# An attention, expert and ELU feed-forward chain: score tiles on both partition halves, paired transposes, smaller softmax joins, values in three parts

## The chip, the core and the metric

The kernel runs on one core of a Trainium2 chip. The metric is the device time of one execution in microseconds. The engines named below are PE (matrix products; PEld is its loading of weights), DVE (VectorE), ACT (ScalarE), POOL (GpSimd) and SP, whose queue issues most of the transfers.

## What is computed

```python
# attention: q, k, v are (2, 8, 1152, 64)
q_pool = q.reshape(B, H, S // 2, 2, D).mean(axis=3)
scores = scale * np.matmul(q_pool, k.transpose(0, 1, 3, 2))
attn = np.exp(scores - np.max(scores, axis=-1, keepdims=True))
attn = attn / (np.sum(attn, axis=-1, keepdims=True) + 1e-09)
x = np.matmul(attn, v)                      # becomes (1152, 512)
# four experts, weighted
for e in range(4):
    out += p[:, e:e + 1] * (np.maximum(x @ w1[e], 0.0) @ w2[e])
# feed-forward with ELU
h = out @ w_in
g = np.where(h > 0.0, h, np.exp(np.minimum(h, 0.0)) - 1.0)
return g @ w_out
```

There are 16 heads; each has 576 pooled queries and 1152 keys. The two dense stages work on 1152 tokens of 512 features.

## The kernel before

**Two stages.** The attention stage comes first; the dense stage (experts, then ELU layer) follows and uses the attention's result as split pairs `XH` and `XL` (a high part and the remainder). This change touches the attention stage alone.

**Pairs and units.** Heads are taken in 8 pairs `p`; `y` (0 or 1) is the head within the pair. The 576 queries of a head are cut so that a unit `(p, u, y)` with `u` from 0 to 8 holds 64 queries: 32 of the lower and 32 of the upper half (`z`). So a pair has 18 units. A unit's scores lie on all 128 partitions as (z, a, 32 queries), where `a` picks one of two halves of the keys, and on 2 x 288 columns (`n`), in two banks' worth of one score buffer `s`. There are three such buffers.

**The steps.** The planner names each step with a letter:

- `k`, `q`, `v`: loads, issued by SP (the first q by ACT); `a` adds the two queries that are pooled, `b` scales them.
- `S` scores (PE, 8 products of 64 rows by 32 columns, 288 keys each); `R` maximum of a unit (DVE); `E` exponential with its row sum (ACT), which reads the score buffer, writes an `e` buffer and frees the score buffer.
- The join. Each query has its keys on two partitions (`a`), so maximum and sum must be joined: `x` copies the partner's numbers across, `y` takes the smaller negated maximum, `Y` the differences, `e` their exponentials, `z` the whole sum, `r` its reciprocal, `g` the factor. A join is made for a group of units at a time.
- `G` multiplies a unit's 576 columns of `e` by its factor (POOL or ACT), `T` transposes it in blocks of 32 into `pt` (DVE), `V` multiplies by the values (PE, 72 products for a group), `O` and `L` write `XH` and `XL` (ACT, DVE).

In the kernel before, the groups are `GROUPS = ((0, 5), (5, 9))`: units 0 to 4 and 5 to 8 of a pair, 10 and 8 units with both heads. Join and values use the same groups. A head `y` sits on partitions 64y to 64y+63 of the k and q tiles, so all 8 products of one unit use one half of PE's rows, and the two column halves `n` of a unit follow one another on the same four tiles of the array. There are 14 `e` buffers, each for one unit.

**What sets the order.** `order_of` simulates the engines with the costs in `STAGES` and the latencies in `LAG`, and writes every step to its engine in the order of the start that it finds. The engines then run their lists strictly in order. What a step waits for is in `attention_ops`: `S` needs a score buffer freed by an `E`; `E` needs an `e` buffer freed by the `T` of 14 units earlier; `V` needs all `T` of its group; the `T` of a group needs the `V` of the same group one pair earlier. At the end of the stage four blocks of the first dense product (`1`, with `2` and `3` behind it) are mixed in; the planner's tail and `h`, `f` (conversion of the first weights) belong to the same list.

Of the kernel before, what the change touches and what calls it, by code (L numbers as in the profile page):

```python
# [18 lines left out]
P = 128  # L19
# [8 lines left out]
    "q": (dict(SP=500), 0),  # L28
    "k": (dict(SP=500), 0),
    "v": (dict(SP=1000), 2),  # L30
    "a": (dict(POOL=830, DVE=470), 0),
    "b": (dict(ACT=440, POOL=500), 0),
    "S": (dict(PE=560), 0),
    "R": (dict(DVE=750), 0),
    "E": (dict(ACT=960), 0),
    "x": (dict(ACT=860), 0),
    "y": (dict(DVE=175), 0),
    "Y": (dict(POOL=450), 0),
    "e": (dict(ACT=220), 0),
    "z": (dict(POOL=680), 0),  # L40
    "r": (dict(DVE=180), 0),
    "g": (dict(POOL=220), 0),
    "G": (dict(POOL=760, ACT=700), 0),
    "T": (dict(DVE=670), 1),
    "V": (dict(PE=5200), 0),
    "O": (dict(ACT=420), 0),
    "L": (dict(DVE=340), 0),
# [11 lines left out]
NU = 9  # L59
NE = 14  # L60
NG_ST = 4
GROUPS = ((0, 5), (5, 9))

# [4 lines left out]
def attention_ops(NP):  # L68
# [15 lines left out]
    for p in range(NP):  # L84
        b = 2 * NU * p
        old = [("S", *u) for u in units(p - 2)] if p > 1 else []
        for z in (0, 1):
            op(b - 20, old, "k", p, z, after=1000 * z)
            op(b - 20, old, "q", p, z, after=1000 * z)
            op(b - 14, [("q", p, z)], "a", p, z)  # L90
            op(b - 14, [("a", p, z)], "b", p, z)
        for y in (0, 1):
            op(b - 10, [("V", *g) for g in groups(p - 2)] if p > 1 else [], "v", p, y, after=4000)
        for gi, (lo, hi) in enumerate(GROUPS):
            g = (p, gi)
            r = 2 * NU * p + 2 * hi
            old = groups(p - 1)[gi] if p else None
            us = units(p, gi)
            for u in us:
                r0 = b + 2 * u[1] + u[2]  # L100
                op(r0, [(x, p, z) for x in "kb" for z in (0, 1)], "S", *u)
                op(r0, [("S", *u)] + ([("g", *old)] if old else []), "R", *u)
                before_e.append(u)
                op(r0, [("R", *u)] + ([("T", *before_e[-1 - NE])] if len(before_e) > NE else []), "E", *u)
            op(r, [("E", *u) for u in us], "x", *g)
            op(r, [("x", *g)], "y", *g)
            op(r, [("y", *g)], "Y", *g)
            op(r, [("Y", *g)], "e", *g)
            op(r, [("e", *g)], "z", *g)
            op(r, [("z", *g)], "r", *g)  # L110
            op(r, [("r", *g)], "g", *g)
            for j, u in enumerate(us):
                op(r + 0.9 * j, [("g", *g)], "G", *u)
                op(r + 0.9 * j, [("G", *u)] + ([("V", *old)] if old else []), "T", *u)
            op(r + 8, [("T", *u) for u in us] + [("v", p, y) for y in (0, 1)], "V", *g)
            for z in (0, 1):
                op(r + 8, [("V", *g)], "O", *g, z)
                op(r + 8, [("O", *g, z)], "L", *g, z)
# [18 lines left out]
def order_of(ops):  # L137
# [12 lines left out]

    while ready:
        best = []
        for o, t in ready.items():
            x = takes.get(o[0])
            if x:
# [3 lines left out]
            _, e = min((max(t, free[e]) + n, e) for e, n in STAGES[o[0]][0].items())  # L159
# [3 lines left out]
        free[e] = start + STAGES[o[0]][0][e]  # L163
        end[o] = free[e] + LAG[e]
        x, bank = takes.get(o[0]), None
        if x:
# [8 lines left out]
        elif o[0] == "L" and ("L", *o[1:3], 1 - o[3]) in end:  # L175
            back = ("V", *o[1:3])
# [13 lines left out]
def attention_then_moe_then_elu_ffn(  # L190
# [124 lines left out]
    with ExitStack() as actx:  # L315
# [13 lines left out]
        et = [e_p.tile([P, CB * 32], F32, name="e%d" % j) for j in range(NE)]  # L329
# [7 lines left out]
        def load_k(e, p, z):  # L337
            if p not in kt:
                kt[p] = kq_p.tile([P, KC * P], F32, tag="k", name="k")
            t = kt[p][:, z * KQ : z * KQ + KQ]  # L340
            for y in (0, 1):
                r = slice(64 * y, 64 * y + 64)
                if p == 0:
                    nc.sync.dma_start(out=t[r], in_=qk0[4 * y + 2 * z + 1, r])
                else:
                    src = kT[p // HP, p % HP].rearrange("(z d) y s -> z y d s", z=2)
                    nc.sync.dma_start(out=t[r], in_=src[z, y])  # L347

        def load_q(e, p, z):
            if p not in qs:  # L350
                qs[p] = kq_p.tile([P, 2, 2, HQ], F32, tag="q", name="q")
            t = qs[p][:, z].rearrange("p m s -> p (m s)")
            for y in (0, 1):
                r = slice(64 * y, 64 * y + 64)
                if p == 0:
                    nc.scalar.dma_start(out=t[r], in_=qk0[4 * y + 2 * z, r])
                else:
                    src = qT[p // HP, p % HP].rearrange("(z d) y m s -> z y d (m s)", z=2)
                    nc.sync.dma_start(out=t[r], in_=src[z, y])

        def load_v(e, p, y):
            vt[p, y] = t = v_p.tile([P, CB, D], F32, tag="v%d" % y, name="v")
            src = v[p // HP, 2 * (p % HP) + y].rearrange("(r t) c d -> r (t c d)", t=2)
            for z in (0, 1):
                nc.sync.dma_start(
                    out=t[64 * z : 64 * z + 64].rearrange("p b d -> p (b d)"), in_=src
                )

        def q_sum(e, p, z):
            a, b = qs[p][:, z, 0], qs[p][:, z, 1]  # L370
# [397 lines left out]
```

## Time and profile before

| | us |
|---|---|
| median of 3 runs | 922.22 (922.06 to 929.28) |
| profiled execution | 926.59 |
| its span, first to last instruction | 924.8 |
| PE busy | 870.4 |
| DVE busy | 508.4 |
| POOL busy | 473.2 |
| ACT busy | 337.7 |
| mean granted clock of TensorE, share of full | 0.924 |

The span is what the rows further down are measured in. A busy PE counts every moment in which some product is in flight, at either clock.

### The profile page before, as it was taken

What the parts mean: (1) busy time and instruction counts of PE and PEld (TensorE: products, weight loads), DVE (VectorE), ACT (ScalarE), POOL (GpSimd) and SP (SyncE); (2) the same over time, 40 slices, a digit from 0 to 9 for tenths busy, and PEclk for the clock granted to TensorE, in tenths of its full rate; (3) what the DMA queues carried; (4) which work ended last, traced back from release to release, by engine and by line L of the source; (5) the groups of instructions that cost most, each with busy time, mean ns of one, the idle gap of its engine ahead of it and who ended that gap; (6) DMA issues with size and microseconds to landing.
All of it is one profiled execution on the core that took longest, in us unless ns stands there. A gap on an engine that the chain in (4) does not pass through costs nothing.

```text
span 924.8 us, 19138 instructions
## 1 busy us (share of the span) xinstructions
PE 870.4 (94%) x8182; PEld 761.3 (82%) x8182; DVE 508.4 (55%) x729; ACT 337.7 (37%) x698; POOL 473.2 (51%) x417
## 2 busy tenths in 40 slices
PE   7698798987978899999999999999999999999998
PEld 4365454654645799999999999999999999999998
DVE  3757676677776615655655646556465732333332
ACT  4656565556675422212222122221222253313211
POOL 0648556586674734354556364646546462534511
PEclk7777976979778899999999999999999999999999
DMA  8112213122240053233243331513333231000001
GB/s 205 54 28 79 52 54 96 48 67 53 82 116 2 1 209 114 94 108 120 80 146 108 99 130 42 186 62 124 104 114 115 88 116 46 1 1 1 1 35 69
DMA packets 24341, 75.20 MB, mean 81 GB/s; under 512 B 3904, under 2 KB 6464, under 8 KB 21312
## 3 DMA queue, kind: packets, MB, share of 16 engines
q1 hardware_dynamic: 23936, 73.38, 25.6%
q8 instruction: 64, 1.05, 0.5%
q10 hardware_dynamic: 320, 0.59, 0.3%
q14 instruction: 21, 0.17, 0.1%
HBM read 63.20 MB, written 10.77 MB: 80 GB/s over the span
## 4 chain that ended last, share of the span: by engine, by line
PE 79%; DVE 7%; POOL 7%; ACT 3%; issue 2%; DMA 1%; SPq 1%; ACTq 0%; DVEq 0%
PE p L283 59%; PE v L495 9%; PE s L407 9%; POOL e L479 5%; DVE st L417 3%; ACT e L428 2%; PE s L283 2%; DVE pt L483 1%; POOL acc L668 1%; DMA q<-in_q 1%; DVE XL L238 1%; DMA k<-in 1%; SPq L347 0%; DVE nt L597 0%; ACT XH L617 0%
## 5 line engine op out<-in xcount | busy, mean ns | idle before, releaser
L407 PE MATMUL s<-k,q 64*32 64x288 f32 x2304 | 171.1, 512 | 46.9 <-ACT e L428 42.8
L283 PE MATMUL p<-hh,h 128*128 128x384 f32 (+1 forms) x592 | 195.3, 330 | 1.6 <-DVE hl L311 1.6
L283 PE MATMUL p<-hh,l 128*128 128x384 f32 (+1 forms) x592 | 195.2, 330 | 0.0
L283 PE MATMUL p<-hl,h 128*128 128x384 f32 (+1 forms) x592 | 195.2, 330 | 0.0
L283 PE MATMUL p<-XH,h 128*128 128x384 f32 (+1 forms) x560 | 185.9, 332 | 0.4 <-DVE e L643 0.4
L283 PE MATMUL p<-XL,h 128*128 128x384 f32 (+1 forms) x560 | 185.8, 332 | 0.0
L283 PE MATMUL p<-XH,l 128*128 128x384 f32 (+1 forms) x560 | 185.8, 332 | 0.0
L407 PEld LDWEIGHTS s<-k,q 64*32 64x32 f32 x2304 | 67.3, 121 | 140.6 <-ACT e L428 86.1
L238 POOL TENSOR_TENSOR l<-w,h 128x512 fp32r<-128x512 f32 x96 | 125.5, 1324 | 85.5 <-ACT h L235 85.5
L479 POOL TENSOR_SCALAR e<-e,df 128x576 f32<-128x576 f32 x87 | 148.3, 1724 | 1.7
L307 ACT ACTIVATE hh<-p 128x768 fp32r<-128x768 f32 (+1 forms) x46 | 36.8, 801 | 277.7 <-PE p L283 277.7
L428 ACT ACTIVATE e<-s,st 128x576 f32<-128x576 f32 x144 | 106.1, 738 | 83.0 <-DVE st L417 76.2
L417 DVE TENSOR_REDUCE st<-s 128x1 f32<-128x576 f32 x144 | 104.4, 733 | 40.1 <-PE s L407 35.5
L483 DVE STREAM_TRANSPOSE pt<-e 128x576 f32<-128x576 f32 x144 | 107.9, 763 | 28.4 <-POOL e L479 15.0
L311 DVE SCALAR_TENSOR_TENSOR hl<-p,hh 128x768 fp32r<-128x768 f32 (+1 forms) x46 | 43.2, 940 | 144.1 <-ACT hh L307 144.1
L283 PEld LDWEIGHTS p<-hh,h 128*128 128x128 f32 x592 | 111.1, 188 | 1.8 <-POOL l L238 1.8
L283 PEld LDWEIGHTS p<-hl,h 128*128 128x128 f32 x592 | 111.1, 188 | 0.0
L283 PEld LDWEIGHTS p<-hh,l 128*128 128x128 f32 x592 | 111.1, 188 | 0.0
L283 PEld LDWEIGHTS p<-XH,h 128*128 128x128 f32 x560 | 105.1, 188 | 0.7 <-PE p L283 0.7
L283 PEld LDWEIGHTS p<-XL,h 128*128 128x128 f32 x560 | 105.1, 188 | 0.0
L283 PEld LDWEIGHTS p<-XH,l 128*128 128x128 f32 x560 | 105.1, 188 | 0.0
L612 POOL TENSOR_TENSOR nt<-nt,ne 128x512 f32<-128x512 f32 x32 | 41.8, 1306 | 121.8 <-issue 61.5
(61 smaller groups left out, 902.7 us busy)
## 6 DMA issues: line engine op xcount, KB each, us to landing
v<-in_v SPq DMA_DIRECT2D x32, 288.0 KB, 5.1
w<-in_wb SPq DMA_DIRECT2D x8, 1024.0 KB, 6.6
d<-in_va SPq DMA_DIRECT2D x16, 512.0 KB, 4.3
w<-nt SPq DMA_DIRECT2D x32, 256.0 KB, 3.4
d<-in_vb SPq DMA_DIRECT2D x16, 512.0 KB, 4.2
w<-w SPq DMA_DIRECT2D x8, 1024.0 KB, 6.4
w<-in_wa SPq DMA_DIRECT2D x7, 1024.0 KB, 7.2
k<-in_k SPq DMA_DIRECT2D x28, 144.0 KB, 2.9
```

What stands on the lines that cost most here:

```text
L238: engines[e].tensor_tensor(out=out, in0=a, in1=b, op=op)
L283: nc.tensor.matmul(out=ps, lhsT=w[:, c, m * P : m * P + P], rhs=x[:, c], start=c == 0 and w is hi and x is xh, stop=c == 3 and w is lo,)
L307: nc.scalar.activation(halves(g, n, m)[0], ps[:, :, : n[1]], AF.Relu)
L311: nc.vector.scalar_tensor_tensor(out=ol, in0=ps[:, :, : n[1]], scalar=0.0, in1=f(oh), op0=ALU.max, op1=ALU.subtract)
L407: nc.tensor.matmul(out=t[o : o + 32, n, : CB * 16], lhsT=qs[p][r, z, 0, 32 * u : 32 * u + 32], rhs=k[:, :, a, :, n], start=True, stop=True,)
L417: nc.vector.tensor_reduce(out=st[j][:, 0, i : i + 1], in_=s_t[p, u, y][:, :, : CB * 16], axis=AX.XY, op=ALU.max, negate=True,)
L428: nc.scalar.activation(t.rearrange("p (n k) -> p n k", n=2), s_t.pop((p, u, y))[:, :, : CB * 16], AF.Exp, bias=st[j][:, 0, i : i + 1], acc ...
L479: engines[e].tensor_scalar(out=t, in0=t, scalar1=x, scalar2=None, op0=ALU.mult)
L483: nc.vector.transpose(pt[g][:, :, y, u - GROUPS[g][0], :], place.pop((p, u, y)).rearrange("p (b c) -> p b c", c=32),)
L495: nc.tensor.matmul(out=v_bank[z][64 * y : 64 * y + 64, :m], lhsT=vt[p, y][r, b], rhs=pt[g][r, b, y].rearrange("p u c -> p (u c)"), start=b ...
L612: nc.gpsimd.tensor_tensor(out=t, in0=t, in1=e, op=ALU.add)
L668: nc.gpsimd.tensor_tensor(out=o, in0=o, in1=t, op=ALU.add)
```

## The change

The edits, all in the attention stage:

- **k and q tiles.** The partition half is now the key half `n`, not the head. A k tile holds head `y` in its second dimension; q is needed on both partition halves and is loaded twice, so a pair's q comes by 8 transfers of 64 partitions instead of 4, and its k by 2 of 128 partitions instead of 4 of 64. `a` and `b` now handle 576 columns for a head. `b` is ACT's alone. The first pair's q is issued by SP.
- **S.** The 8 products of a unit go to 8 different tiles of 64 rows by 32 columns.
- **T.** One transpose handles both heads of a `u` (1152 columns); there are 7 `e` buffers of two units.
- **Join.** Groups for the join are `STATS`, 2, 3, 2 and 2 values of `u` (4 to 6 units), while values keep the two `GROUPS`. `x` moves from ACT to POOL; `Y` and `z` lose an operation each. There are 32 joins instead of 16.
- **G.** On POOL it is a product of two tensors with a broadcast factor instead of a product with a scalar. Which engine takes a unit is fixed: 8 of the 18 units of a pair on ACT, 10 on POOL (over the whole stage 64 and 80; it was 57 and 87).
- **V.** A group's 72 products come in three parts, each a step of its own for the planner.

```diff
 STAGES = {
-    "S": (dict(PE=560), 0),
+    "S": (dict(PE=600), 0),
...
-NE = 14
-NG_ST = 4
+NE = 7
+NG_ST = 8
+NV = 3
+GS = 9
+GA = (1, 3, 5, 7)
 GROUPS = ((0, 5), (5, 9))
+STATS = ((0, 2), (2, 5), (5, 7), (7, 9))
...
+            for j in range(NV):
+                need = [("V", *g, j - 1)] if j else [("T", *u[:2]) for u in us] + [("v", p, y) for y in (0, 1)]
+                op(r + 8, need, "V", *g, j)
...
+    def of(o):
+        if o[0] == "G":
+            e = "ACT" if (2 * o[2] + o[3]) % GS in GA else "POOL"
+            return {e: STAGES["G"][0][e]}
+        return STAGES[o[0]][0]
...
+                    src = qT[p // HP, p % HP, part(z), y].rearrange("d m s -> d (m s)")
+                    for n in (0, 1):
+                        nc.sync.dma_start(out=t[part(n)], in_=src)
...
-            r = slice(64 * y, 64 * y + 64)
-            k = kt[p][r].rearrange("p (c a r n) -> p c a r n", c=KC, a=2, n=2)
-            for n in (0, 1):
-                for z in (0, 1):
-                    for a in (0, 1):
-                        o = 32 * (2 * z + a)
+            k = kt[p][:, y].rearrange("p (i a r) -> p i a r", a=2, r=32)
+            for z in (0, 1):
+                for a in (0, 1):
+                    o = 32 * (2 * z + a)
+                    for n in (0, 1):
                         nc.tensor.matmul(
                             out=t[o : o + 32, n, : CB * 16],
-                            lhsT=qs[p][r, z, 0, 32 * u : 32 * u + 32],
-                            rhs=k[:, :, a, :, n],
+                            lhsT=qs[p][part(n), y, z, 0, 32 * u : 32 * u + 32],
+                            rhs=k[part(n), :, a],
...
-                nc.scalar.copy(
+                copy(
+                    e,
...
-            tt(e, d[:, 0], d[:, 1], s[:, 0], ALU.subtract)
-            tt(e, d[:, 1], d[:, 1], s[:, 1], ALU.subtract)
+            tt(e, d[:, :2], d[:, 2:].to_broadcast([P, 2, d.shape[2]]), s[:, :2], ALU.subtract)
...
-                engines[e].tensor_scalar(out=t, in0=t, scalar1=x, scalar2=None, op0=ALU.mult)
+                tt(e, t, t, x.to_broadcast([P, CB * 32]), ALU.mult)
...
-        def transposes(e, p, u, y):
+        def transposes(e, p, u):
             g = group_of(u)
             nc.vector.transpose(
-                pt[g][:, :, y, u - GROUPS[g][0], :],
-                place.pop((p, u, y)).rearrange("p (b c) -> p b c", c=32),
+                pt[g][:, :, :, u - GROUPS[g][0], :],
+                place[p, u].rearrange("p y (b c) -> p b y c", c=32),
             )
 
-        def values(e, p, g, n):
+        def values(e, p, g, j, n=None):
...
-            for b in range(CB):
+            for b in range(CB * j // NV, CB * (j + 1) // NV):
```

The order that results on PE: before, a pair is 12 units of scores, all of `V` of group 0, 6 units, all of `V` of group 1. Now it is (from pair 3 on) 10 units, a third of `V` of group 0, a unit, a third, a unit, a third, 4 units, and then group 1's thirds with a unit after the first and after the second.

On DVE, in pair 3, where group 1 (`pt_107` before, `pt_100` now) is transposed and the values of group 0 are written out. Before:

```order
L483 STREAM_TRANSPOSE pt_107<-e_104 128x18x32
L483 STREAM_TRANSPOSE pt_107<-e_105 128x18x32
L483 STREAM_TRANSPOSE pt_107<-e_92 128x18x32
L238 TENSOR_TENSOR XL<-v_111,XH 128x160
L238 TENSOR_TENSOR XL<-v_112,XH 128x160
L483 STREAM_TRANSPOSE pt_107<-e_93 128x18x32
L417 TENSOR_REDUCE st_115<-s_109 128x1
L483 STREAM_TRANSPOSE pt_107<-e_94 128x18x32
L417 TENSOR_REDUCE st_115<-s_110 128x1
```

Now:

```order
L490 STREAM_TRANSPOSE pt_100<-e_98 128x36x32
L425 TENSOR_REDUCE st_111<-s_101 128x1
L490 STREAM_TRANSPOSE pt_100<-e_92 128x36x32
L474 RECIPROCAL st_109<-st_109 128x4
L252 TENSOR_TENSOR df_118<-st_110 128x4
L425 TENSOR_REDUCE st_111<-s_102 128x1
L252 TENSOR_TENSOR XL<-v_104,XH 128x160
L252 TENSOR_TENSOR XL<-v_105,XH 128x160
L425 TENSOR_REDUCE st_111<-s_103 128x1
L490 STREAM_TRANSPOSE pt_100<-e_93 128x36x32
```

The maxima (`TENSOR_REDUCE`) of new units now stand between the transposes and around the `XL` steps, where four transposes had no maximum between them before; a join's small steps (`RECIPROCAL`, `df<-st`) stand among them too.

On POOL, at a join of pair 3. `df` and `st` hold a join's numbers, the lines with `e` are `G`, the line with `q` is `a` and (L378) `b`. Before:

```order
L479 TENSOR_SCALAR e_99<-e_99,df_119 128x576
L238 TENSOR_TENSOR df_120<-df_120,st_116 128x8 x2
L238 TENSOR_TENSOR q<-q 128x288
L238 TENSOR_TENSOR st_116<-st_116,df_120 128x8 x2
L238 TENSOR_TENSOR st_116<-st_116 128x8
L238 TENSOR_TENSOR st_116<-st_116,eps 128x8
L378 TENSOR_SCALAR q<-q 128x288 x2
L238 TENSOR_TENSOR df_120<-df_120,st_116 128x8
L479 TENSOR_SCALAR e_101<-e_101,df_120 128x576
```

Now:

```order
L249 COPY st_112<-st_112 32x2x4 x4
L252 TENSOR_TENSOR e_93<-e_93,df_119 128x576
L252 TENSOR_TENSOR e_94<-e_94,df_119 128x576
L252 TENSOR_TENSOR e_95<-e_95,df_119 128x576
L252 TENSOR_TENSOR df_120<-df_120,st_112 128x2x4
L252 TENSOR_TENSOR e_95<-e_95,df_119 128x576
L252 TENSOR_TENSOR st_112<-st_112,df_120 128x2x4
L252 TENSOR_TENSOR st_112<-st_112 128x4
L252 TENSOR_TENSOR st_112<-st_112,eps 128x4
L249 COPY st_113<-st_113 32x2x4 x4
L252 TENSOR_TENSOR q<-q 128x2x288
L252 TENSOR_TENSOR df_120<-df_120,st_112 128x4
```

The copies `x` (L249) are new on POOL, and the `G` of one join stand between the steps of the next one.

## Rows read from the trace of the kernel before

**Rows 1.** Busy time by engine: attention stage, then the rest.

```profile
0.00:328.17 328.17, 279.36 (x4703) 171.17 (x4703) 218.86 (x368) 185.66 (x468) 191.93 (x227) 0.79 0.25 66
328.17:924.80 596.63, 590.99 (x3481) 590.17 (x3480) 289.58 (x361) 152.03 (x230) 281.25 (x190) 1.00 0.27 90
```

**Rows 2.** The same for one pair; columns: length, PE, PEld, DVE, ACT, POOL, PEclk, DMA.

```profile
162.37:169.05 6.68, 6.68 (x153) 6.22 (x157) 3.54 (x6) 3.05 (x7) 5.97 (x7) 0.75 0.02 7
169.05:176.13 7.08, 5.83 (x100) 2.26 (x102) 6.73 (x12) 4.43 (x11) 3.03 (x2) 1.00 0.01 2
176.13:180.22 4.09, 4.09 (x151) 3.92 (x154) 1.29 (x3) 2.65 (x10) 0.47 (x3) 1.00 0.01 4
180.22:190.60 10.38, 6.21 (x114) 2.67 (x113) 7.48 (x13) 6.44 (x15) 8.44 (x10) 0.95 0.47 116
190.60:199.25 8.65, 8.65 (x84) 3.22 (x87) 7.62 (x13) 5.79 (x17) 5.41 (x6) 0.50 0.46 128
```

**Rows 3.** The chain that ended last: start, length, what (all us).

```profile
44.68 7.46 PE v L495 x144
...
272.15 6.62 PE v L495 x144
...
306.28 9.35 PE s L283 x48
315.63 5.05 PE v L495 x144
320.68 3.40 PE s L283 x24
```

**Rows 4.** Timeline: start, length, engine, line, operation, tile, count.

```profile
12.87 2.08 DVE L417 TENSOR_REDUCE st<-s 128x1 f32<-128x576 f32 x3
...
194.01 1.18 SPq L359 DMA_DIRECT2D q<-in_q  x2
...
202.98 2.11 ACT L477 ACTIVATE e<-e,df 128x576 f32<-128x576 f32 x3 [1.97 <-POOL df L238]
...
206.17 2.24 PE L407 MATMUL s<-k,q 64*32 64x288 f32 x48
...
211.06 0.76 DVE L483 STREAM_TRANSPOSE pt<-e 128x576 f32<-128x576 f32 x1
...
211.75 0.72 DVE L417 TENSOR_REDUCE st<-s 128x1 f32<-128x576 f32 x1
...
212.12 1.22 PE L407 MATMUL s<-k,q 64*32 64x288 f32 x16 [0.16 <-ACT e L428]
212.39 0.76 DVE L483 STREAM_TRANSPOSE pt<-e 128x576 f32<-128x576 f32 x1
...
250.94 0.74 ACT L428 ACTIVATE e<-s,st 128x576 f32<-128x576 f32 x1 [0.43 <-DVE st L417]
...
251.67 0.73 ACT L428 ACTIVATE e<-s,st 128x576 f32<-128x576 f32 x1
...
329.24 5.00 POOL L238 TENSOR_TENSOR l<-w,h 128x512 fp32r<-128x512 f32 x4 [7.47 <-ACT h L235]
```

**Rows 5.** Groups of POOL's instructions by line and shape: count, busy, mean ns.

```profile
L479 POOL TENSOR_SCALAR e<-e,df 128x576 f32<-128x576 f32 x11 | 18.7, 1723 | 0.2
...
L238 POOL TENSOR_TENSOR st<-st,df 128x10 f32<-128x10 f32 x2 | 0.4, 208 | 0.3 <-ACT df L456 0.3
...
L668 POOL TENSOR_TENSOR acc<-acc,t 128x768 f32<-128x768 f32 x42 | 76.6, 1846 | 0.0
```

**Rows 6.** Busy time in stretches of 2 us, columns as in rows 2.

```profile
96.00:98.00 2.00, 1.83 (x28) 0.55 (x20) 2.00 (x4) 1.51 (x4) 0.00 (x0) 0.84 0.00 0
...
190.00:192.00 2.00, 1.40 (x12) 0.57 (x16) 1.72 (x3) 1.07 (x3) 2.00 (x2) 0.50 0.00 0
...
198.00:200.00 2.00, 2.00 (x24) 0.97 (x20) 1.11 (x2) 0.95 (x4) 1.25 (x4) 0.50 0.62 191
...
204.00:206.00 2.00, 2.00 (x68) 1.94 (x60) 1.76 (x3) 1.09 (x2) 2.00 (x2) 1.00 0.03 8
```

More of the change, by code (lines that the diff above doesn't have):

```diff
@@ L27 @@
 STAGES = {
-    "q": (dict(SP=500), 0),
+    "q": (dict(SP=1000), 0),
     "k": (dict(SP=500), 0),
     "v": (dict(SP=1000), 2),
-    "a": (dict(POOL=830, DVE=470), 0),
-    "b": (dict(ACT=440, POOL=500), 0),
-    "S": (dict(PE=560), 0),
[L34 to L38, printed above, removed]
-    "e": (dict(ACT=220), 0),
[L40 to L47, printed above, removed]
+    "a": (dict(POOL=1440, DVE=700), 0),
+    "b": (dict(ACT=730), 0),
+    "S": (dict(PE=600), 0),
+    "R": (dict(DVE=735), 0),
+    "E": (dict(ACT=935), 0),
+    "x": (dict(POOL=820), 0),
+    "y": (dict(DVE=170), 0),
+    "Y": (dict(POOL=240), 0),
+    "e": (dict(ACT=220), 0),
+    "z": (dict(POOL=640), 0),
+    "r": (dict(DVE=200), 0),
+    "g": (dict(POOL=210), 0),
+    "G": (dict(POOL=1440, ACT=770), 0),
+    "T": (dict(DVE=1370), 1),
+    "V": (dict(PE=1600), 0),
+    "O": (dict(ACT=290), 0),
+    "L": (dict(DVE=310), 0),
     "l": (dict(SP=730), 20),
@@ L327, in attention_then_moe_then_elu_ffn @@
         kt, qs, vt = {}, {}, {}
-        et = [e_p.tile([P, CB * 32], F32, name="e%d" % j) for j in range(NE)]
+        et = [e_p.tile([P, 2, CB * 32], F32, name="e%d" % j) for j in range(NE)]
         pt = [e_p.tile([P, CB, 2, hi - lo, 32], F32, name="pt%d" % j) for j, (lo, hi) in enumerate(GROUPS)]
@@ L335, in group_of, with part, load_k @@
             return next(j for j, (lo, hi) in enumerate(GROUPS) if lo <= u < hi)
-        def load_k(e, p, z):
+        def part(n):
+            return slice(64 * n, 64 * n + 64)
+        def load_k(e, p, y):
             if p not in kt:
-                kt[p] = kq_p.tile([P, KC * P], F32, tag="k", name="k")
-            t = kt[p][:, z * KQ : z * KQ + KQ]
-            for y in (0, 1):
-                r = slice(64 * y, 64 * y + 64)
+                kt[p] = kq_p.tile([P, 2, KQ], F32, tag="k", name="k")
+            t = kt[p][:, y]
+            if p == 0:
+                for n in (0, 1):
+                    nc.sync.dma_start(out=t[part(n)], in_=qk0[4 * y + 2 * n + 1, part(n)])
+            else:
+                nc.sync.dma_start(out=t, in_=kT[p // HP, p % HP][:, y])
@@ L369, in q_sum @@
-        def q_sum(e, p, z):
-            a, b = qs[p][:, z, 0], qs[p][:, z, 1]
-            tt(e, a, a, b, ALU.add)
-        def q_scaled(e, p, z):
-            a = qs[p][:, z, 0]
-            if e == "ACT":
-                nc.scalar.activation(a, a, AF.Copy, scale=SCALE)
-            else:
-                engines[e].tensor_scalar(out=a, in0=a, scalar1=SCALE, scalar2=None, op0=ALU.mult)
-        NS = 2 * max(hi - lo for lo, hi in GROUPS)
+                nc.sync.dma_start(out=t[part(z)], in_=src)
@@ L382, in attention_then_moe_then_elu_ffn, with q_sum, q_scaled @@
+        def q_sum(e, p, y):
+            a, b = qs[p][:, y, :, 0], qs[p][:, y, :, 1]
+            tt(e, a, a, b, ALU.add)
+        def q_scaled(e, p, y):
+            a = qs[p][:, y, :, 0]
+            nc.scalar.activation(a, a, AF.Copy, scale=SCALE)
+        NS = 2 * max(hi - lo for lo, hi in STATS)
         st = [mx_p.tile([P, 4, NS], F32, name="st%d" % j) for j in range(NG_ST)]
-        df = [mx_p.tile([P, 2, NS], F32, name="df%d" % j) for j in range(NG_ST)]
+        df = [mx_p.tile([P, 3, NS], F32, name="df%d" % j) for j in range(NG_ST)]
```

118 lines of the change are left out of this document (53 added, 65 removed).

## The prediction

> **What bounds the kernel now.** I first read the busy time of the two stages [rows 1]. The dense stage, 596.6 us, has PE busy for 591.0 at the full clock, and no edit touches it. The attention stage takes 328.2 us, and none of its engines is full: PE is busy 279.4, DVE 218.9, POOL 191.9, ACT 185.7, at a mean granted clock of 0.79. So it is bounded by engines waiting for one another, and the question is which waits the change removes.
>
> Next I read the chain that ended last. The values of group 0 start at 44.68 in pair 0 and at 272.15 in pair 6 [rows 3]: 227.5 us for six pairs, 37.9 a pair. Then I cut one pair into five stretches by this chain [rows 2]: the values of group 0 (6.68 us), a stretch in which DVE alternates transposes and maxima (7.08), the values of group 1 (4.09), a stretch with POOL busy 8.44 of 10.38, and five units of scores at half the clock (8.65). The fullest engine over the pair is DVE: 3.54 + 6.73 + 1.29 + 7.48 + 7.62 = 26.7 of 36.9 us. Of its 10.2 idle us, 3.1 + 2.8 lie in the two values steps, where PE makes no scores and DVE soon has nothing left to reduce; 2.9 lie in the POOL stretch, where the `e` buffers are full until POOL has multiplied (1.723 us a unit, 11 of the 18 units in rows 5) and DVE has transposed; 1.0 lies in the last stretch.
>
> **The change, engine by engine, for one pair.** Everything that changes runs beside something else, so I sum each engine and then look for the stretch in which each is last.
>
> DVE: a maximum followed by a transpose takes 0.64 and a transpose followed by a maximum 0.69 from start to start [rows 4]. A transpose of two heads costs at most two of the old ones, 1.38, and at least that less the fixed part, which I take as under 0.1. Nine of them for 18 save 0 to 0.9. Two more joins add two `y` and two `r`, small steps of about 0.2 like POOL's 0.208 [rows 5]: 0.8. So 26.7 becomes 26.6 to 27.5; I take 27.
>
> POOL: no row shows the product with a broadcast factor. The nearest are products of two tensors: 512 columns in 1.25 (four in 5.00) [rows 4], 768 in 1.846 [rows 5], between them 1.40 for 576. The other end is the old 1.723. I take 1.40, since only the shape differs. Ten `G` are 14.0; four joins of nine small steps at 0.2 are 7.2, of which the copies `x` (16) are new on POOL; one `a` of 576 columns is 1.4: 22.6 us, against 23.3 before (the sum of rows 2). With 1.723 it would be 26.2, still below DVE.
>
> ACT: 22.4 before. It loses eight copies (-1.6), gains one `G` (0.70, three in 2.11 [rows 4]), two `b` of 576 columns (1.4) and two `e` (0.4): 23.3.
>
> PE: alone, a unit takes 1.22 [rows 4], two sets of four products one after the other on the same four tiles. Units of the two heads already overlap, since they use different row halves: three in 2.24, 0.75 each [rows 4]. So the change gives back-to-back units little and a lone unit much. A lone one is between 0.61 (half of 1.22) and 1.22; I take 0.9, for one set plus its loading and its tail. The values are 5.05 [rows 3] and 4.09 [rows 2] at the full clock. The stretch with the values now holds six thirds, four lone units between them and a run of four: 9.1 + 3.6 + 3.0 = 15.7. The clock is not full there at first: it is 0.50 in the late score stretch even with PE busy without a gap (198 to 200), and 1.00 only some us after the values begin [rows 6]; the step at 44.68 took 7.46 for 5.05 [rows 3]. I add 2.5 once a pair: 18.2.
>
> The TensorEngine Tiling page of the Trainium skill (Key Properties) says that changing the tiling mode, not just the tile, drains TensorE. Here the mode changes twelve times a pair instead of four. The trace shows no gap at a change: the values that start at 315.63 end 5.05 later, at 320.68, where the next product of another shape starts [rows 3]. If each of the eight new changes cost an estimated 0.25 beyond my lone units, the time would be 12 us higher, 875.
>
> Transfers: a pair's q is 8 transfers instead of 4, its k 2 instead of 4; two issues take 1.18 on SP [rows 4], so the ten take about 6 us where eight took 4.7. They start when the last unit two pairs back is done, and the second head's `a` on DVE comes about nine us later by the row of its list; the last of the ten needs its issue and then some us to land, so 0 to 1.5 us a pair of waiting is possible. `v` loads and the next pair's stand behind them on SP, and have a whole pair's time. I take 0.5, which is inside my rounding.
>
> **The sum of a pair.** Two stretches follow one another. In the one without values, ten to eleven units pass: ACT has 11 exponentials at 0.73 [rows 4], four `G` at 0.70, two `b` and two `e`, 12.6 us; DVE has about 12 there. In the one with values PE has 18.2 and DVE about 15. That is 30.8; I take 31.0. It is 4 above DVE's own sum, because the numbers of each smaller join still cross engines seven times, between engines that run strictly in order. The join itself leaves the path: a group of 4 to 6 units now waits for the last of these, not for the tenth, and seven double `e` buffers cover 14 units, so the stall in the POOL stretch (2.9) should go. What is late next is PE in the values stretch.
>
> **The edges.** Start: the first scores need only the first head's k and q, so I put the first maximum three us before 12.87 [rows 4], at 10. Up to the first values DVE has 22 maxima (14.5), five double transposes (6.8) and 2 of small work, 23.3, and I allow 3.5 for waits: 37, not 44.68 (bounds 34 and 44). Then 6 x 31 = 186: the values of pair 6 start at 223. From there DVE does 11 maxima (7.2), six double transposes (8.1) and small steps (1.6) before the last scores; with a tenth for waits and 2.4 for the exponential that frees a buffer, the dense blocks start at 244. PE then has 9.35 for two of them, 5.05, two more of 3.40, and 4.09 [rows 2, 3]: 25.3, so the last values end at 269. Before, they ended at 328.17 [rows 1]. Behind them the order differs, the last dense block now stands ahead of the values, but it bought nothing there: the next product had to wait for POOL's four conversions, 5.00 us from 329.24 [rows 4], longer than the block.
>
> The gain is 328.2 - 269.3 = 59 us. Against the profiled execution that is a span of 924.8 - 59 = 866, an execution of 926.6 - 59 = 868; against the median, which lies 4.4 below the profiled one, **863 us**.
>
> **Rivals.**
>
> 1. *DVE becomes the only bound.* The lists leave enough slack that a pair costs 27.5 to 29. Six pairs at 28 instead of 31 give 845. For it: DVE has ready work in every stretch. [...]
> 2. *The eight tiles don't run at once.* Then the change doesn't do what it says: a unit is 1.22 wherever it stands alone, and about 2 at half the clock. The values stretch becomes 9.1 + 8 x 1.22 + 2.5 = 21.4, the other about 13.5 (1.35 a unit): 34.9 a pair, 23 us more, 886. Against it: units of the two heads overlap across the row halves in rows 4.
> 3. *The join chain is late.* With POOL's `G` at 1.723 and transfers late by 1.5, a pair's lists slip against one another, ACT's `G` blocks the exponentials behind it, and a pair costs 34 to 35: 881 to 887.
> 4. *Slower: PE stays at half the clock.* The thirds are cut by scores that wait for a buffer, so the clock, which before rose inside the long values steps, never rises. Then the values are 18.2 and 18 units about 1.3 each, 23.4: 41.6 a pair, and the tail's 25.3 becomes about 43. First values at 40, pair 6 at 290, the end near 354: 26 us later than now, 948. It decides from a pair of 38 up, that is PE at half the clock for about eight tenths of its work.
>
> On that rival the TensorE: Matmul & The Clock Gate page of the Trainium skill (Loop structure matters more than you think) says that the loop nest decides whether matmuls run at the upper level, and that waits between bursts drop it. The trace agrees that scores at DVE's pace do not hold the clock [rows 6]. It also shows the clock back at full some five us after the values begin, and a third followed by one lone unit is still nearly gapless work, so I give the rival little.
>
> **How the numbers follow.** Forecast (29.3 to 33 us a pair, 852 to 876): 0.50. Rival 1 (836 to 852): 0.20. Rivals 2 and 3 together (876 to 905): 0.20. A gain mostly lost elsewhere, 905 to 931: 0.06. Rival 4: 0.04. The range of 840 to 888 leaves a part of rival 1 and the upper part of rivals 2 and 3 out. Of this kernel a measurement tells about 1% (9 us) from no change. Faster by more than that, below 913: 0.90; within it: 0.05; slower: 0.05.
>
> **What would show it.** Right: in the trace after, two starts of the values of group 0 are 29 to 33 us apart; a lone unit of scores takes 0.8 to 1.0 at the full clock; DVE is busy over 80% between the first and last values; the dense stage is 596 us as before. Wrong: units of 1.2 or more at the full clock (rival 2); exponentials that wait for POOL or for `G` ahead of them on ACT (rival 3); a granted clock near 0.5 through the values (rival 4); `a` on DVE waiting for transfers of q. A double transpose above 1.5, or a broadcast product on POOL above 1.8, would make my sums too small.

## The result, and the profile after

The changed kernel takes **880.02 us** (median of 3 runs, 878.35 to 882.16) against 922.22: 0.952 of the time before (95% interval 0.9445 to 0.9596). Forecast was 863, so the sign and the range of 840 to 888 held, and the size was 17 us too good. The profiled execution is one of 878.35 with a span of 876.5. One execution of joins_large, a kernel further down, took 1578.12 us where its others took 881.02 to 887.74, and is left out of its median.

First the two stages, then the six pairs from the first values of pair 0 to those of pair 6, then pair 3 in four stretches: values of group 0 with units between them, maxima and transposes, values of group 1, and units alone. Columns as in [rows 2].

```profile
0.00:278.05 278.05, 208.29 (x4726) 123.62 (x4726) 220.35 (x329) 179.18 (x441) 160.66 (x384) 0.91 0.37 95
278.05:876.50 598.45, 591.45 (x3456) 589.68 (x3456) 288.95 (x360) 151.28 (x229) 281.26 (x190) 0.99 0.27 89
44.82:232.74 187.92, 142.92 (x3456) 80.40 (x3456) 163.75 (x246) 131.15 (x329) 120.83 (x282) 0.92 0.38 95
137.11:142.60 5.49, 5.49 (x140) 4.03 (x132) 3.07 (x5) 3.82 (x9) 4.58 (x6) 0.89 0.32 75
142.60:149.95 7.35, 4.83 (x120) 2.44 (x113) 7.35 (x13) 5.32 (x14) 4.32 (x15) 0.91 0.01 2
149.95:155.00 5.05, 5.05 (x136) 3.94 (x128) 4.35 (x5) 3.71 (x8) 3.17 (x7) 0.79 0.02 3
155.00:167.94 12.94, 8.59 (x216) 3.27 (x208) 11.65 (x21) 8.79 (x24) 7.67 (x21) 1.00 0.79 190
```

All of the gain is in the attention stage: 328.17 before [rows 1], 278.05 now. A pair takes 187.92 / 6 = 31.3 us instead of 37.9, DVE is busy 87% of that, and the clock is 0.92 (0.79 over the whole stage before). The dense stage is 1.8 longer.

The chain of waits from the values of pair 6 on (start, length, what), as [rows 3]:

```profile
232.76 1.85 PE v L502 x48
234.60 0.65 PE s L415 x16
235.25 1.79 PE v L502 x48
237.04 0.65 PE s L415 x16
237.69 1.80 PE v L502 x48
...
254.18 6.58 PE s L297 x48
260.77 1.79 PE v L502 x48
262.56 3.40 PE s L297 x24
...
273.67 4.40 PE v L502 x144
```

A lone unit of scores between two thirds takes 0.65 in this chain; a lone unit took 1.22 before [rows 4]. Thirds and units follow one another without a gap.

The start, timeline of DVE and of SP's queue:

```profile
5.83 2.39 SPq L374 DMA_DIRECT2D q<-in_q  x4
...
8.26 3.22 SPq L380 DMA_DIRECT2D v<-in_v  x4
...
10.22 2.08 DVE L425 TENSOR_REDUCE st<-s 128x1 f32<-128x576 f32 x3
11.53 0.59 SPq L362 DMA_DIRECT2D k<-in_k  x1
12.16 2.65 SPq L374 DMA_DIRECT2D q<-in_q  x4
13.12 0.76 DVE L425 TENSOR_REDUCE st<-s 128x1 f32<-128x576 f32 x1 [0.82 <-PE s L415]
15.51 4.55 SPq L380 DMA_DIRECT2D v<-in_v  x4
22.22 0.76 DVE L252 TENSOR_TENSOR q<-q 128x576 f32<-128x576 f32 x1 [8.34 <-DMA q<-in_q]
```

The first maximum is at 10.22. After the fourth, DVE stands for 8.34 us in front of `a` of pair 1's second head, in order: that q was issued at 12.16, behind a load of `v`, and lands at 22. The maxima behind it have long been ready. In steady pairs it is the same in small. The groups of `q` over the six pairs (engine and operation: us waited for the transfer, times), and two of the waits on DVE:

```profile
  DVE q L252: 10.8, 5
  POOL q L252: 8.9, 4
...
DMA to landing us min/median/max: 2.8/5.1/6.5
```

```profile
140.55 0.90 DVE L252 TENSOR_TENSOR q<-q 128x576 f32<-128x576 f32 x1 [2.42 <-DMA q<-in_q]
...
171.89 0.76 DVE L252 TENSOR_TENSOR q<-q 128x576 f32<-128x576 f32 x1 [2.56 <-DMA q<-in_q]
```

The 2.42 lie inside pair 3's values of group 0, where DVE is busy 3.07 of 5.49. What DVE didn't do there it does behind them, and then it is busy 7.35 of 7.35 while PE has work for 4.83.

POOL's products and copies and DVE's two largest groups over the six pairs, as [rows 5]:

```profile
L252 POOL TENSOR_TENSOR e<-e,df 128x576 f32<-128x576 f32 x59 | 68.1, 1174 | 1.2
L249 POOL COPY st<-st 32x8 f32<-32x8 f32 x71 | 13.6, 191 | 4.0 <-ACT df L464 0.6 <-ACT e L436 0.2
```

```profile
L425 DVE TENSOR_REDUCE st<-s 128x1 f32<-128x576 f32 x109 | 78.6, 742 | 8.5 <-PE s L415 8.0
L490 DVE STREAM_TRANSPOSE pt<-e 128x1152 f32<-128x1152 f32 x54 | 72.0, 1354 | 0.9 <-POOL e L252 0.9
```

The product with a broadcast factor takes 1.17 us, not 1.72.

### The profile page after: what moved, and what is told of

Read it like the earlier page. It is cut to its first block, busy times and chain, and to the rows that moved or that the text cites. A ratio compares the mean times of both kernels' runs of the same rounds, so it can differ in the third digit from the quotient of the medians.

```text
span 876.5 us, 19338 instructions
## 1 busy us (share of the span) xinstructions
PE 799.7 (91%) x8182; PEld 713.3 (81%) x8182; DVE 509.3 (58%) x689; ACT 330.5 (38%) x669; POOL 441.9 (50%) x574
## 4 chain that ended last, share of the span: by engine, by line
PE 74%; DVE 8%; DMA 5%; issue 5%; ACT 4%; POOL 3%; SPq 1%; DVEq 0%; ACTq 0%; POOLq 0%
PE p L297 62%; PE v L502 6%; PE s L415 4%; DMA q<-in_q 3%; DVE pt L490 3%; DVE st L425 3%; PE s L297 2%; ACT e L436 1%; ACT e L484 1%; POOL e L252 1%; POOL acc L675 1%; SPq L374 1%; DMA k<-in_k 1%; DMA v<-in_v 1%; DVE XL L252 0%
## 5 line engine op out<-in xcount | busy, mean ns | idle before, releaser
L415 PE MATMUL s<-k,q 64*32 64x288 f32 x2304 | 108.0, 456 | 63.2 <-ACT e L436 61.0
L415 PEld LDWEIGHTS s<-k,q 64*32 64x32 f32 x2304 | 31.4, 111 | 124.0 <-ACT e L436 112.3
L654 POOL TENSOR_TENSOR hl<-e,hh 128x768 fp32r<-128x768 f32 x24 | 44.5, 1853 | 106.9 <-ACT hh L653 106.8
L490 DVE STREAM_TRANSPOSE pt<-e 128x1152 f32<-128x1152 f32 x72 | 96.0, 1355 | 3.1 <-POOL e L252 3.1
```

The lines of the kernel that those rows point to most:

```text
L415: nc.tensor.matmul(out=t[o : o + 32, n, : CB * 16], lhsT=qs[p][part(n), y, z, 0, 32 * u : 32 * u + 32], rhs=k[part(n), :, a], start=True, ...
L490: nc.vector.transpose(pt[g][:, :, :, u - GROUPS[g][0], :], place[p, u].rearrange("p y (b c) -> p b y c", c=32),)
L654: nc.gpsimd.tensor_tensor(out=ol, in0=e, in1=f(oh), op=ALU.subtract)
```

## The experiments

**Theory.** The 50 us of the attention stage come from several edits together: POOL's shorter product, the new tiles, the smaller joins, the thirds. The missing 17 come from q: a sum of q stands too early in DVE's and POOL's lists, at the start and in each pair. **Rivals.** One edit carries the gain; or the pair is bound by DVE and the waits for q cost nothing. Of the change's edits five are undone below; `x` on POOL, the fixed engine of each `G`, `b` on ACT alone and the shorter `Y` and `z` are not.

In the table the starts are those of the first values in each profiled execution; "pairs" is the time from pair 0's to pair 6's, by six; "rest" is from there to the end of the attention stage. Comparison runs of the kernel before had medians of 924.9 to 926.0.

| kernel | median, us | ratio to before, 95% | first values | a pair | rest | stage ends |
|---|---|---|---|---|---|---|
| before | 922.22 | | 44.6 | 37.9 | 56.1 | 328.2 |
| changed | 880.02 | 0.952 (0.945 to 0.960) | 44.8 | 31.3 | 45.3 | 278.1 |
| v_whole | 887.61 | 0.957 (0.950 to 0.963) | 45.8 | 31.8 | 45.7 | 282.2 |
| joins_large | 885.26 | 0.953 (0.946 to 0.960) | 46.0 | 31.2 | 49.0 | 282.0 |
| t_single | 883.28 | 0.955 (0.950 to 0.960) | 45.6 | 31.8 | 45.9 | 282.3 |
| layout_old | 892.49 | 0.961 (0.955 to 0.967) | 44.3 | 33.4 | 49.5 | 294.2 |
| pool_scalar | 898.22 | 0.967 (0.961 to 0.973) | 47.9 | 33.5 | 47.0 | 296.0 |
| pool_and_layout_old | 902.29 | 0.974 (0.966 to 0.982) | 42.2 | 35.2 | 51.4 | 304.8 |
| before_pool | 913.38 | 0.987 (0.981 to 0.994) | 45.5 | 37.0 | 53.3 | 320.7 |
| v_later | 878.46 | 0.949 (0.943 to 0.955) | 41.7 | 32.1 | 45.3 | 279.7 |
| sp_cost | 865.4 | 0.934 (0.930 to 0.938) | 39.3 | 29.9 | 46.3 | 265.2 |
| sp_cost_v | 859.69 | 0.928 (0.923 to 0.934) | 37.5 | 29.5 | 46.3 | 260.9 |
| a_pool | 874.71 | 0.944 (0.939 to 0.948) | 36.1 | 31.8 | 46.1 | 273.1 |
| sp_joins_large | 878.23 | 0.948 (0.944 to 0.952) | 34.9 | 31.7 | 53.8 | 279.1 |

The last four columns come from one execution each, and it can lie off its kernel's median: 5 us below in v_whole, 6 above in before_pool. The changed kernel alone spreads over 3.8 us. So 4 us of the stage are about the least that these runs tell from nothing, and the intervals of the changed kernel, v_whole, joins_large and t_single overlap.

### One part undone

**v_whole**: the values of a group in one piece.

```diff
-    "V": (dict(PE=1600), 0),
+    "V": (dict(PE=4800), 0),
-NV = 3
+NV = 1
```

> The changed kernel with a group's values in one part again (one third of the change's order undone, the list planned anew). If the gain comes from letting scores through between the values and from the small joins, DVE again runs dry during a values step: about 3 us a pair more, 880 becomes about 900, with DVE idle beside the values. If the new score layout is what brought the gain, values in one part cost nothing: 878 to 885.

887.61, between the two ranges. The stage is 4 us longer, which is not clear of the spread. Pairs alternate between 26 and 35 (the last takes 42), with a mean near that of the changed kernel. The idle DVE that was expected didn't come: over six pairs it waits 9.7 us for scores, against 8.0. PE does the whole group in little less than the thirds, which are 1.85 + 1.79 + 1.80 above:

```profile
236.50 5.13 PE v L502 x144
```

**joins_large**: two joins a pair, over the groups of the values.

```diff
-NG_ST = 8
+NG_ST = 4
-STATS = ((0, 2), (2, 5), (5, 7), (7, 9))
+STATS = GROUPS
```

> The changed kernel with joins of 10 and 8 units again (two a pair instead of four). If the small joins removed the stall in which all e buffers are full, it returns with about 2.9 us a pair: about 900, with exponentials that wait for transposes behind POOL. If joins were not the cause (POOL's faster products alone removed the stall), 875 to 885, since 16 fewer joins save POOL about 1.8 us each.

885.26. The stage is 4 us longer, at the start (1.2) and in the rest (3.7), none of it in the pairs, and this too is not clear of the spread. In the prediction a stall of 2.9 a pair went with the smaller joins; by this run alone it did not. sp_joins_large, below, takes the question up again.

**t_single**: two transposes in a row instead of one of two heads.

```diff
-            nc.vector.transpose(
-                pt[g][:, :, :, u - GROUPS[g][0], :],
-                place[p, u].rearrange("p y (b c) -> p b y c", c=32),
-            )
+            for y in (0, 1):
+                nc.vector.transpose(
+                    pt[g][:, :, y, u - GROUPS[g][0], :],
+                    place[p, u][:, y].rearrange("p (b c) -> p b c", c=32),
+                )
```

> The changed kernel with each transpose of two heads issued as two transposes of one head, at the same place of DVE's list. The prediction gave the double form at most 0.1 us a unit, 0.9 a pair. By that 880 to 888. If the double form really saves a fixed part of a few tenths, DVE, which is busy 87% of the stretch of pairs, is 2 us a pair fuller and the time 890 to 896. If the pairs are held by the transfers of q and not by DVE: 880 to 882.

883.28, as the prediction's 0.9 a pair has it, though the time can't be told from that of the changed kernel. DVE's group of transposes over six pairs:

```profile
L491 DVE STREAM_TRANSPOSE pt<-e 128x576 f32<-128x576 f32 x109 | 76.0, 743 | 0.9 <-POOL e L252 0.9
```

76.0 against 72.0: 0.7 a pair.

**layout_old**: tiles, loads and sums of k and q, the order of v's rows and the scores as before.

```diff
-                op(r0, [("k", p, u[2]), ("b", p, u[2])], "S", *u)
+                op(r0, [(x, p, z) for x in "kb" for z in (0, 1)], "S", *u)
...
-                            lhsT=qs[p][part(n), y, z, 0, 32 * u : 32 * u + 32],
-                            rhs=k[part(n), :, a],
+                            lhsT=qs[p][r, z, 0, 32 * u : 32 * u + 32],
+                            rhs=k[:, :, a, :, n],
```

> The changed kernel with the k, q and v tiles and the score products of before (a head on a partition half, four tiles of the array used twice by a unit), everything else as changed. If the order of values and joins made the gain, the lone unit of scores goes back from about 0.72 to 1.2 us, which costs 1 to 2 us a pair, and q comes by half the bytes, which gives back about 2: 875 to 892. If the layout made the gain: 905 to 922.

892.49, just above the first range: 16 us of the stage and 2.1 a pair. The eight tiles do run at once, and that pays where a unit stands alone between thirds; the chain of this kernel, with 1.19 for a unit where the changed kernel has 0.65:

```profile
249.67 1.79 PE v L510 x48
251.46 1.19 PE s L423 x16
```

Over the six pairs DVE waits 28.5 us for scores, against 8.0. This undoes the second copy of q as well (the waits for it fall from 19.7 to 5.4), so the tiles alone may be worth more.

**pool_scalar**: only the form of POOL's product.

```diff
-                tt(e, t, t, x.to_broadcast([P, CB * 32]), ALU.mult)
+                engines[e].tensor_scalar(out=t, in0=t, scalar1=x, scalar2=None, op0=ALU.mult)
```

> The changed kernel with POOL's product by a scalar operand again, 1.72 us a unit by the kernel before, instead of the 1.17 us that the broadcast product now takes. POOL's sum for a pair rises by 10 x 0.55 to about 25 of 31 us. If POOL is not the bound: 882 to 890. If POOL's product was the hidden source of the stall before, the exponentials wait for buffers again and it is 900 or more.

898.22: the most of any single part, 18 us of the stage, 2.2 a pair. The six pairs of this kernel:

```profile
47.92:249.00 201.08, 152.50 (x3457) 86.64 (x3457) 165.79 (x246) 132.29 (x329) 154.62 (x280) 0.87 0.35 88
```

POOL is busy 154.62 instead of 120.83 and still only 77%: it costs through what waits for it, not as the fullest engine. DVE's transposes over the six pairs show the wait:

```profile
L490 DVE STREAM_TRANSPOSE pt<-e 128x1152 f32<-128x1152 f32 x54 | 73.9, 1373 | 14.2 <-POOL e L486 14.1
```

DVE stands 14.1 us in front of transposes whose product isn't done (0.9 in the changed kernel, by its row of L490 above). That is 2.2 a pair more, as much as the pair is longer. The exponentials that were expected to wait for buffers wait 1.6 us for a transpose, as in the changed kernel.

**pool_and_layout_old**: both of these.

> The changed kernel with both of the largest parts undone: POOL multiplies by a scalar factor as before, and the key halves, queries, values and their loads are laid out as before. Undone alone they cost 18 and 12 us against 880. If they are on the path in turn, the sum holds: 907 to 913. If they lie beside each other and one hides the other: 897 to 902. If each only pays when the other is there (a pair takes the longer of POOL's and PE's chain, as a pair of the kernel before does): also near 898, with the period of the pair the same as with POOL's scalar product alone. Above 915 if they hinder each other.

902.29, at the upper end of the range for one hiding the other: 27 us of the stage where the two alone make 16 + 18 = 34. In the pairs they nearly add up (3.9 of 2.1 + 2.2); the start hides the rest, since the first values come at 42.2.

**before_pool**: the kernel before with POOL's product in the new form.

```diff
-                engines[e].tensor_scalar(out=t, in0=t, scalar1=x, scalar2=None, op0=ALU.mult)
+                tt(e, t, t, x.to_broadcast([P, CB * 32]), ALU.mult)
```

> The kernel before with one line changed: POOL multiplies by the factor broadcast along the row, with the same order of instructions on every engine. 11 products a pair become 0.55 shorter each, 6 us of POOL. Theory A (POOL's products hold the e buffers, so the stall of 2.9 a pair in the kernel before comes from them, and the smaller joins and the double buffers were not needed for it): 2.5 to 4 a pair over seven and a half pairs, 893 to 905. Rival B (in the kernel before POOL is not last: group maxima, single transposes and the scores at half clock set the pair): 918 to 926, the gain is only there once the other parts have been changed. My own prediction's account, in which the stall went with the smaller joins, wants B.

913.38, between the ranges of the two theories: 0.9 a pair and 2.8 in the rest. POOL's busy time in its six pairs falls by about a quarter and most of it does nothing. DVE's wait for POOL's products, 10.9 us in the six pairs before, is gone, but its wait for scores rises from 23.0 to 30.7; that the group of ten units, the single buffers and the slow lone unit are what makes the scores late is an argument, not shown. The same edit is worth 18 us by the medians where the other parts are in, and 12 here.

So no part carries the gain alone. Undone alone the five cost 4, 4, 4, 16 and 18 us of the stage, or 8, 5, 3, 12 and 18 by the medians. Only the last two, the layout and POOL's product, are clear of the spread, though layout_old's interval still meets that of the changed kernel.

### The transfers of q

**v_later**: pair 1's second k and q go ahead of v of pair 0 on SP, and in the trace DVE has that sum after three maxima instead of four, so one earlier, not one later as was expected.

```diff
-    "v": (dict(SP=1000), 2),
+    "v": (dict(SP=1000), 12),
```

> The changed kernel with one rank moved: on SP the second head's k and q of pair 1 come ahead of the values of pair 0, and on DVE the sum of that q then stands one maximum later. Theory (the missing gain at the start is DVE standing in order behind the q of pair 1, which is queued behind v): DVE no longer idles some 8 us from 14 to 22, the values of pair 0 start near 38 and not at 44.8, every pair after it as before, 872 to 875 against 880. Rival (the start is held by ACT's and POOL's chain of joins, and DVE would have waited anyway): the values still start at 43 to 45, 878 to 882. A second rival: v now lands too late and the values wait for it; then the chain shows a wait for v before the first values and the time stays at 880.

878.46, not to be told from the changed kernel. The first values come 3.2 earlier, not 6 to 7; q lands five us sooner, but DVE still stands for it:

```profile
17.23 0.76 DVE L252 TENSOR_TENSOR q<-q 128x576 f32<-128x576 f32 x1 [4.51 <-DMA q<-in_q]
```

And what was won is given back: the values of pair 2 start at 106.3, in the changed kernel at 106.8, and those of pair 6 at 234.4 against 232.7. The theory held for the place and failed for the sum. The second head's q of the next pairs is issued 4.0, then 2.3, then 1.8 us earlier (36.90, 69.38 and 101.78, where it was 40.86, 71.67 and 103.60), and DVE and POOL still wait 17.1 us for q in six pairs; why the lead shrinks is not shown.

**sp_cost**: the planner's costs for k and q as the trace shows them. The transfers are the same ones in another order: SP takes v of pair 0's first head ahead of both q of pair 1, which are issued at 8.62 and 14.03 (5.83 and 12.16 in the changed kernel). The sums of q come later in the lists, and 10 of the 12 after 40 us are on DVE, where it was 7.

```diff
-    "q": (dict(SP=1000), 0),
-    "k": (dict(SP=500), 0),
+    "q": (dict(SP=3000), 0),
+    "k": (dict(SP=800), 0),
```

> The changed kernel with only the planner's costs of q (3.0 us) and k (0.8) set to what the trace shows; v keeps its rank, so SP still takes v of pair 0 ahead of pair 1's second k and q, while the list of DVE now puts the sum of that q later. Theory (what counts is where the sum of q stands in DVE's and POOL's order, not when the transfer is issued): nearly all that the version with v ranked later gained, 859 to 864. Rival (the order of the transfers on SP itself counts): the first pair still starts at 43 to 45 and only the gain within the pairs is left, 866 to 871.

865.4. Just above the theory's 859 to 864 and just under the rival's 866 to 871. The mark that separates them is the start: 39.3, where the rival has 43 to 45. The sum of pair 1's second q stands after ten maxima instead of four:

```profile
22.41 0.76 DVE L252 TENSOR_TENSOR q<-q 128x576 f32<-128x576 f32 x1 [0.91 <-DMA q<-in_q]
```

It starts when it did (22.22), so q is no earlier, but the wait is 0.91 and not 8.34 (the first q's sum, now on DVE too, waits 3.36). So at the start the place of the sum in the list counts. In the pairs two things changed at once, the place of the sums and their engine.

**sp_cost_v**: this, and v at its cost and ranked later.

```diff
-    "q": (dict(SP=1000), 0),
-    "k": (dict(SP=500), 0),
-    "v": (dict(SP=1000), 2),
+    "q": (dict(SP=3000), 0),
+    "k": (dict(SP=800), 0),
+    "v": (dict(SP=2000), 12),
```

> The changed kernel with the planner's costs for transfers set to what the trace shows (q 3.0 us for its four issues, k 0.8, v 2.0) and v ranked later, so that the planner puts the sums of q later on DVE and POOL. Theory (a pair of the changed kernel still pays some 2 us for q that hasn't landed, and the start 6 to 7): the start as in v_later, and 1 to 2 us less in each of six pairs: 862 to 868. Rival (the waits for q are hidden by the values, which bound the pair): only the start, 872 to 875. Worse than the changed kernel (over 882) if the later sums delay the first scores of a pair.

859.69, the fastest version: 7.3 at the start, 10.8 in six pairs, against the changed kernel. Its six pairs, and the same sum of q at the start:

```profile
37.50:214.65 177.15, 136.23 (x3425) 78.03 (x3425) 164.30 (x248) 129.58 (x324) 116.63 (x277) 0.94 0.38 100
```

```profile
18.14 0.76 DVE L252 TENSOR_TENSOR q<-q 128x576 f32<-128x576 f32 x1 [1.76 <-DMA q<-in_q]
```

No engine waits for a transfer of q between the first values and those of pair 6 any more (19.7 us before this edit), 8.34 at the start have become 1.76, and DVE is busy 93%. The number of transfers and their bytes are unchanged; 11 of the 12 sums of q in the pairs are now on DVE, where it was 7.

### What bounds the fastest version

**a_pool**: sp_cost_v with the sums of q on POOL alone.

```diff
-    "a": (dict(POOL=1440, DVE=700), 0),
+    "a": (dict(POOL=1440), 0),
```

> The version with the transfers' costs set right (859.7) and the sums of q given to POOL alone, which takes 1.41 us each there instead of 0.73 on DVE: DVE is busy 93% of its pairs of 28.8 us, POOL 66%. Theory (with the waits for q gone, DVE is the bound, so 1.4 us a pair less on it shortens the pair): 28.0 to 28.3 a pair, 850 to 856. Rival (the wait for q comes back, now on POOL, which stands in order before the products and the joins): 862 to 875.

874.71. The theory fell: DVE is busier than any other engine, yet taking work from it made the pair 2.3 longer. The number lies with the rival, its reason doesn't: no sum of q waits for a transfer between 40 and 240. What the trace shows are waits across engines. Three pairs of a_pool (98.86 to 191.37), then three of sp_cost_v (99.3 to 185.91); engine and what it waited for, us, times, longest:

```profile
ACT XH L516 <- PE v L502: 13.3, 6, 2.5
...
POOL st L252 <- ACT df L464: 10.7, 6, 1.9
...
DVE st L425 <- PE s L415: 4.8, 10, 0.8
```

```profile
ACT XH L516 <- PE v L502: 4.7, 3, 1.6
...
POOL st L252 <- ACT df L464: 3.8, 6, 1.0
...
DVE st L425 <- PE s L415: 1.2, 1, 1.2
```

ACT stands 4.4 us a pair in front of `O` for values that aren't done, with exponentials behind it, where it stood 1.6. Whether that comes from the 0.7 more that a sum takes on POOL or from the other lists that the planner made, this run doesn't tell. It does limit what sp_cost_v shows: with no wait for q in the pairs here either, a pair takes 31.8, no less than the changed kernel's 31.3. So the pairs of sp_cost_v may owe their 1.8 us to the sums that moved from POOL to DVE as well as to the waits that went. The start doesn't: it is early here too (36.1).

**sp_joins_large**: sp_cost_v with two joins a pair.

```diff
-NG_ST = 8
+NG_ST = 4
-STATS = ((0, 2), (2, 5), (5, 7), (7, 9))
+STATS = GROUPS
```

> The version with the transfers' costs set right (859.7) with two joins a pair again instead of four. In the changed kernel itself that cost 6 us, all of it at the start and in the tail and none in the pairs, where the waits for q may have covered it. Theory (the smaller joins take a stall out of the pairs, once nothing else covers it): 1 to 2 us more in each pair, 870 to 880. Rival (seven double buffers are enough for the larger joins, and the smaller ones only help the ends): 862 to 867; below 860 if the small operations that are saved on DVE, 0.9 a pair, count for more.

878.23, in the theory's range: the same edit that cost 4 us of the stage in the changed kernel costs 18 here, 2.2 in each pair and 7.5 in the rest. The six pairs' waits:

```profile
POOL st L249 <- ACT e L436: 52.4, 11, 8.6
...
DVE st L425 <- PE s L415: 24.3, 18, 2.4
```

POOL stands up to 8.6 us in front of a join for the last exponential of its group, 52.4 in all (11.7 in sp_cost_v), and DVE waits 24.3 for scores (7.8 in sp_cost_v). In joins_large the same two waits are 52.1 and 22.5, against 7.1 and 8.0 in the changed kernel, while the waits for q fall from 19.7 to 6.2: there one wait seems to have stood in for the other. How POOL's wait makes the scores late is argued, not shown. It is not the stall that the prediction named, in which the `e` buffers are full: exponentials wait 0.4 us for a transpose in these six pairs. Not tried: a shorter transfer of q, by one copy or a third pair of its buffers.

## Why the prediction was right, and where it was off

- **Period**: 31.0 forecast, 31.3 measured. In pair 3 the two stretches are 17.9 and 12.9, forecast 18.2 and 12.6. That this is so close is in part luck, since inside them terms cancelled. PE was to be last in the stretch with values; in the middle 7.35 us of it DVE was busy throughout and PE for 4.83. POOL's product is 1.17, below both bounds I had taken (1.40 and 1.723), so POOL needs 20.1 a pair, not 22.6; the 1.40 fits a sum of two full tensors (1.41), not this product. (With 1.723 my terms make 25.8, not the 26.2 that I wrote; pool_scalar has 154.62 / 6 = 25.8.) A lone unit is 0.65 to 0.72, not 0.9. The clock's 2.5 was real in part: in pair 3 the score stretch is at full clock now, and 0.79 to 0.91 is granted in the stretches with values. I had read from [rows 6] that scores at DVE's pace do not hold the clock; they can, since [rows 2] has 1.00 from 169.05 to 176.13, where DVE is busy 6.73 of 7.08. Against that stand the waits for q, which I had put at 0.5 with a bound of 1.5: 19.7 us on two engines in six pairs. Without them a pair is 29.5 in sp_cost_v, 1.8 less, but 31.8 in a_pool, so their price is not known by itself. DVE's 27.3 a pair is as forecast (27), and so is its 87% (over 80).
- **The stall of 2.9**: I read it as full `e` buffers. In the six pairs before, ACT's idle time in front of its exponentials is 63.5 us, 61.8 of it for maxima and none for a transpose. What the trace has is DVE standing in order for products that aren't done:

```profile
DVE pt L483 <- ACT e L477: 11.1, 5, 2.8
DVE pt L483 <- POOL e L479: 10.9, 26, 0.9
```

That is 3.7 a pair; in the changed kernel it is 0.9 us in all six pairs together. So the wait went, but it was another than I named.

- **Start**: the term that failed, 37 against 44.8. The first maximum came where I put it (10 against 10.22). Then I counted DVE's work and 3.5 for waits; one wait alone, for a transfer of q, was 8.34. I had named `a` on DVE waiting for q as a sign of failure and costed it in steady pairs only. sp_cost_v starts at 37.5, which shows what the 37 lacked.
- **Rest**: 46.3 forecast, 45.3 measured. The dense stage, which I held equal, is 1.8 longer: the chain there goes through a transfer of weights (4.06 from 278.62), and PE is granted 0.50, the 1.2 GHz level, from 282 to 288. Which of these makes the 1.8 is not shown.
- **The sum**: 7.8 at the start, 1.9 in the pairs, -1.0 in the rest, 1.8 in the dense stage make 10.5 of span. The other 6 are the offset that I carried over from profiled execution to median: -4.4 before, +1.7 after.
- **Which edit pays**: the engine sums didn't show it. I let POOL's product weigh nothing, since POOL would be below DVE at either price; undone it costs 18 us, and DVE stands 14.1 us for it in the six pairs.
- **Rivals**: units of 1.2 (rival 2) and half the clock (rival 4) didn't come. Rival 1's period of 27.5 to 29 is nearly that of sp_cost_v. Of rival 3 the late transfers came; POOL's 1.723 didn't. The 880 lies in the interval of 876 to 905 that I gave to rivals 2 and 3 with 0.20, not in my own of 852 to 876, though the period is my own and the largest part of the loss is at the start.

On the changes between tiles of 64x32 and 64x64, the rows show no gap: three thirds and two units take 6.74 from 232.76, and thirds cost 0.3 more than the whole (5.44 against 5.13), all at the full clock. The 0.25 a change that the prediction weighed has no row behind it. The TensorEngine Tiling (Array Packing) page of the Trainium skill (Key Properties) has the mode change drain TensorE; no row here shows such a drain by itself.

On q's two copies the SBUF — State Buffer page of the Trainium skill (Can I just issue two DMAs to hit both halves?) says that two transfers to the two partition halves go hardly faster than one after the other. The median from issue to landing agrees in direction, 5.1 us here and 3.0 in layout_old with half the transfers; but it is 4.2 in sp_cost_v with as many, and no run isolates it.

## What to carry to other kernels

A step that waits for a transfer must not stand in an in-order list ahead of work that is ready: ask for each such step at the start and in the steady state when its transfer was issued and what is behind it; giving a planner the measured cost of the transfers of q and k was worth 15 us here, and 20 with the cost and rank of v, part of it perhaps by the engine that the sums went to. An engine that is not full can still set the time through its latency in a chain, so undo a part before believing a busy sum. And a part's worth depends on the others: the same edit to the joins cost 4 us under another wait and 18 without it.

## What the runs showed of the hardware

- On POOL a product of 576 columns with a factor broadcast along the row takes 1.17 us, with a scalar operand 1.72, and the sum of two full tensors of the same size 1.41.
- Small operations and sums on DVE vary in length: `df` of 4 columns took 0.11 to 1.12 us in the changed kernel, and the sum of q on DVE, as a median after 40 us, 0.73 in sp_cost_v and 1.43 in sp_joins_large; maxima and transposes keep their time (0.74, 1.35). What does it was not tried.
- The clock was granted in full (2.4 GHz) from 155.00 to 167.94, with PE busy 8.59 of 12.94; in the last stretch of [rows 2] it was at 0.50 (1.2 GHz) with PE busy 8.65 of 8.65.
